# Products with V in two runs of three key tiles per unit, and the probabilities' copies split in halves

## The chip, the cores and the metric

One core of a Trainium2 chip. The metric is the time of one execution in device microseconds: the median of several runs. Beside the runs there is one execution with the hardware profiler on; its rows are what this document reads. PE is TensorE's matmul, PEld its weight load, DVE is VectorE, ACT is ScalarE, POOL is GpSimd, SP is SyncE. Lines (L406) are those of the kernel's file before the change.

## What is computed

A clustered attention and two feed-forward layers, one after the other. Only the first matters here:

```python
def _attn_ref(q, k, v, centroids):          # 2 batches, 8 heads, 768 positions, head width 64
    q_assign = np.argmax(np.einsum('bhsd,hcd->bhsc', q_n, c_n), axis=-1)
    k_assign = np.argmax(np.einsum('bhsd,hcd->bhsc', k_n, c_n), axis=-1)
    mask = q_assign[:, :, :, None] == k_assign[:, :, None, :]
    scores = scale * np.matmul(q, k.transpose(0, 1, 3, 2))
    scores = np.where(mask, scores, -1000000000.0)
    scores = scores - np.max(scores, axis=-1, keepdims=True)
    attn = np.exp(scores)
    attn = attn / (np.sum(attn, axis=-1, keepdims=True) + 1e-09)
    return np.matmul(attn, v)
```

Behind it, each token goes to one of eight experts (`moe`, 512 to 1024 to 512), and the result through a dense layer (`moe2`, 512 to 2048 to 512).

## The kernel before

The attention is cut into **units**: a unit is one pair of heads and one half (384) of the 768 query positions, so there are 2 x 4 x 2 = 16. A unit has six **steps**, one per head of the pair and per 128 queries (`part`, line 356). The loop at line 685 runs over all 96 steps and writes the order of the work out by hand; each engine takes its instructions in that order. For step `s` of the loop:

- `scores(s + 1)` (line 359): four matmuls on TensorE into `psS`, two for each stretch of keys (512 and 256 columns); lines 367 and 368 hold the product and the mask's part. `psS` has two buffers.
- `av(u - 1, [i])` (line 402): the products with V of the unit before, one **key tile** (128 of the 768 keys) per step, both heads, accumulated in `psO` over the six steps of a unit. In the trace these are four instructions of line 406 per key tile. After the sixth, `av_evac` (line 409) has ScalarE copy `psO` out (line 414).
- `rowmax(s + 1)` (line 372): VectorE's maximum over the 768 scores (line 374).
- `transp(s - 1)` (line 389): TensorE transposes the 128 x 768 probabilities in six 128 x 128 pieces into `psT` (line 396); then ScalarE copies the first four out (line 399), VectorE the last two (line 400). `psT` has one buffer.
- `softmax(s + 1)` (line 376): ScalarE's exponential with its row sum (line 384), which frees the buffer of `psS`.
- then whatever `todo` holds for that step: the preparation of the next pair of heads (`sim_pair` line 289, `simmax_pair` 301 with line 305 on TensorE and 307 on VectorE, `eqt_pair`, `first_pair`, `mask_pair`, VectorE's subtraction `qlo_pair` line 263, POOL's subtraction line 270), and, at steps 53 and 65 on, the routing of finished tokens (`Route`, line 419, with a product at line 456 and row transposes at line 536).

Unit 0 has no unit before it, so its steps have no products. Step 91 makes all six key tiles of unit 14 in one run (line 694). The last unit's products come in pieces of 128 queries near the end (lines 703, 733, 738).

All of PSUM is one tile `PS` of 4096 columns, eight stretches of 512:

```python
    PS = ps_a.tile([P, 4096], F32, name="PS")
    psS = [PS[:, 1024 * i:1024 * i + S] for i in range(2)]
    psT = PS[:, 2048:2048 + S]
    psO = PS[:, 3072:3072 + CH]
    psM = PS[:, 3584:4096]
```

So key tiles 0 to 3 of `psT` are columns 2048 to 2559, one stretch, and tiles 4 and 5 are in the next. `psM` is the scratch stretch of the preparation and the routing.

Of the kernel before, what the change touches and what calls it, by code (L numbers as in the profile page):

```python
# [14 lines left out]
AF = mybir.ActivationFunctionType  # L15
# [64 lines left out]
def tile_cluster_attention_moe(ctx: ExitStack, tc: tile.TileContext, qk, kk, v, cen, cenr, gate, mw, m2w,  # L80
                               alpha, consts, table, pos, zeros, out):
    nc = tc.nc
# [233 lines left out]
    def eqt_pair(p, hh=None):  # L316
        rs, _, ps = alone(p, hh)
        oh = pre["ohc"][1]
        pb = ps.bitcast(BF16)
        for t in range(3):  # L320
            nc.tensor.transpose(pb[rs, t * P:(t + 1) * P], oh[:, t * P + rs.start:t * P + rs.stop], idb)
        nc.scalar.activation(once("eT", p, [P, CH], BF16)[rs], pb[rs, :CH], AF.Copy)

    def first_pair(p, hh=None):
        rs, _, ps = alone(p, hh)
        eT = pre["eT"][1]
        if hh is not None:

            st, r0 = sets[p % 2], rs.start
            pk = (psT, psM)[hh]  # L330
            nc.tensor.matmul(pk[r0:r0 + 48, :CH], firstb[rs, r0 + NC:r0 + NC + 48], eT[rs], start=True, stop=True)
            nc.tensor.matmul(ps[rs, :CH], firstb[rs, rs], eT[rs], start=True, stop=True)
            for c in range(2):
                cs = slice(c * CH, (c + 1) * CH)
                r1 = r0 + 32 * c
                nc.scalar.activation(st["QB"][64:80, hh, cs], ps[r1:r1 + 16, :CH], AF.Relu)
                nc.vector.tensor_scalar(st["KB"][64:80, hh, cs], pk[r1:r1 + 16, :CH], 0.0, -NEG, ALU.is_le, ALU.mult)
            return
        nc.tensor.matmul(psM[:, :CH], firstb, eT, start=True, stop=True)
        pre["fr"] = ep.tile([P, CH], F32, name=f"fr_{p}", tag="fr")  # L340
        nc.scalar.activation(pre["fr"], psM[:, :CH], AF.Relu)
# [14 lines left out]
    def part(u, i):  # L356
        return (i % 3, i // 3) if u == 0 else divmod(i, 2)

    def scores(s):
        u, i = divmod(s, 6)  # L360
        qt, hh = part(u, i)
        p, c = divmod(u, 2)
        st = sets[p % 2]
        q0 = c * CH + qt * P
        ps = psS[s % 2]
        for ks in (slice(0, 512), slice(512, S)):
            nc.tensor.matmul(ps[:, ks], st["QA"][:, hh, q0:q0 + P], st["KA"][:, hh, ks], start=True, stop=False)  # L367
            nc.tensor.matmul(ps[:, ks], st["QB"][0:96, hh, q0:q0 + P], st["KB"][0:96, hh, ks], start=False, stop=True)  # L368
# [3 lines left out]
    def rowmax(s):  # L372
        smt[s] = sp.tile([P, 1], F32, name=f"sm_{s}", tag="sm")
        nc.vector.tensor_reduce(smt[s], psS[s % 2], AX.X, ALU.max, negate=True)  # L374

    def softmax(s):
        u, i = divmod(s, 6)
        qt, hh = part(u, i)
        p, c = divmod(u, 2)
        b, pr = divmod(p, NPAIR)  # L380
        tt = b * 6 + c * 3 + qt
        h = 2 * pr + hh
        Pt = pp.tile([P, S], F32, name=f"P_{s}", tag="P")
        nc.scalar.activation(Pt, psS[s % 2], AF.Exp, bias=smt.pop(s)[:, 0:1], accum_out=RS[:, tt, h:h + 1])  # L384
        Pts[s] = Pt

    PTs, OTt = {}, {}

    def transp(s):
        u, i = divmod(s, 6)  # L390
        qt, hh = part(u, i)
        Pt = Pts.pop(s)
        if i == 0:
            PTs[u] = ptp.tile([P, 2, KT, CH], F32, name=f"PT_{u}", tag="PT")
        for kt in range(KT):
            nc.tensor.transpose(psT[:, kt * P:(kt + 1) * P], Pt[:, kt * P:(kt + 1) * P], idf)  # L396
        v3 = psT.rearrange("p (k q) -> p k q", k=KT)
        qs = slice(qt * P, (qt + 1) * P)
        nc.scalar.activation(PTs[u][:, hh, 0:4, qs], v3[:, 0:4], AF.Copy)  # L399
        nc.vector.tensor_copy(PTs[u][:, hh, 4:6, qs], v3[:, 4:6])  # L400

    def av(u, kts, qs=slice(0, CH)):
        V = Vt[u // 2]
        for kt in kts:
            for hh in range(2):
                nc.tensor.matmul(psO[64 * hh:64 * hh + 64, qs], V[:, kt, 64 * hh:64 * hh + 64],  # L406
                                 PTs[u][:, hh, kt, qs], start=kt == 0, stop=kt == KT - 1)

    def av_evac(u, qs=slice(0, CH)):
        p, c = divmod(u, 2)  # L410
        b, pr = divmod(p, NPAIR)
        if (b, c) not in OTt:
            OTt[b, c] = otp.tile([P, NPAIR, CH], F32, name=f"OT_{b}_{c}", tag="OT")
        nc.scalar.activation(OTt[b, c][:, pr, qs], psO[:, qs], AF.Copy)
# [139 lines left out]
    def weave(*chains):  # L554

        def steps(parts):
            for f, *a in parts:
                g = f(*a)
                if hasattr(g, "__next__"):
                    yield from g  # L560
                yield
        left = [steps(c) for c in chains]
        while left:
            left = [g for g in left if next(g, left) is not left]
# [59 lines left out]
    U = NU - 1  # L624
# [60 lines left out]
    for s in range(NS):  # L685
        u, i = divmod(s - 1, 6)
        if s + 1 < NS:
            scores(s + 1)
        if 0 < u < U:
            av(u - 1, [i])  # L690
            if i == 5:
                av_evac(u - 1)
        elif u == U and i == 0:
            av(u - 1, range(KT))
            av_evac(u - 1)
        if s + 1 < NS:
            rowmax(s + 1)
        if s == 0:
            eqt_pair(0, 1)
            first_pair(0, 1)  # L700
        if s == NS - 3 or s == NS - 1:
            qs = slice((s - NS + 3) // 2 * P, (s - NS + 5) // 2 * P)
            av(U, range(KT), qs)
            av_evac(U, qs)
        if s > 0:
            transp(s - 1)
        if s + 1 < NS:
            softmax(s + 1)
        for f, a in todo.get(s, []):
            weave([(f, *a)])  # L710
        if s == NS - 5:
            ra = Route(1, 0, 0, 3, 2)
            weave([(ra.inv,), (ra.logits3,)])
        if s == NS - 4:
            weave([(ra.turn,), (ra.max,), (ra.exp,)])
        if s == NS - 3:
            weave([(ra.hot,)])
        if s == NS - 2:
            rb, rc = Route(1, 1, 0, 2, 3), Route(1, 1, 2, 3, 4, bank(1))
            ra.rankmm()  # L720
            ra.rowmm(0, bank(0))
            ra.rowmm(1, bank(1))
            weave([(ra.rankev,)], [(ra.gate,), (rb.inv,)])
            weave([(ra.rowev, 0, bank(0)), (ra.scatter, 0), (ra.rowev, 1, bank(1)), (ra.scatter, 1)])
    qs = slice(2 * P, CH)
    ra.rowmm(2, bank(2))
    rb.logits(ks=[0])
    rb.logits(ks=[1])
    weave([(rb.max,)])
    transp(NS - 1)  # L730
    rb.exp()
    rc.logits([0, 1, 2])
# [459 lines left out]
```

## Time and profile before

| | us |
|---|---|
| three runs: median (lowest to highest) | 749.64 (747.15 to 750.23) |
| the profiled execution: its time | 750.04 |
| its span, first to last instruction | 748.3 |
| what lies around the span | 1.74 |
| TensorE busy | 731.0 |
| VectorE busy | 408.3 |
| ScalarE busy | 291.0 |

The page gives busy times over the whole span. The attention loop ends at about 262 us; the expert and dense layers fill the rest. A row of a timeline gives the start in us, the duration of the (merged) instructions, engine, line, operation, output and inputs, shapes, how many, and in brackets the engine's idle time before it and what ended that. Ends of matmuls are modelled and neighbours overlap, so what a group of matmuls costs is read from start to start.

### The profile page before, as it was taken

The numbers are of one execution on the slowest core, as the hardware profiler recorded it, in microseconds if no ns is written. First come the engines' busy times: TensorE is split into PE (matmuls) and PEld (weight loads), VectorE is DVE, ScalarE is ACT, GpSimd is POOL, SyncE is SP. The second block draws the span as 40 slices with busy tenths as digits, with TensorE's granted clock in tenths as the row PEclk, the third lists the DMA queues.
The fourth block names the chain that finished last, engine by engine and source line by source line (L and its number), as shares of the span: only waits on it lengthen the run. The fifth ranks groups of instructions, "written<-read, shape, count | busy, mean of one in ns | idle before, by whom it ended". The sixth has DMA issues, their size and how long they took to land. (4 is left out here: it accounts for less than half of the span.)

```text
span 748.3 us, 10731 instructions
## 1 busy us (share of the span) xinstructions
PE 731.0 (98%) x4102; PEld 590.8 (79%) x4102; DVE 408.3 (55%) x774; ACT 291.0 (39%) x592; POOL 65.1 (9%) x69
## 2 busy tenths in 40 slices
PE   7999999999999999999999999799999999999996
PEld 2666666666666789999999999688888888888885
DVE  6866767677766540443423335499946343544332
ACT  3877777767666412222322223333312111211111
POOL 5120220222300120000000000000002000020002
PEclk8999999999999999999999999899999999999999
DMA  8265466343420037799786987233201000010001
GB/s 263 54 197 178 146 228 203 87 133 78 157 67 0 30 102 241 205 268 243 278 282 203 278 244 271 63 106 101 75 0 55 4 0 1 0 57 1 0 1 56
DMA packets 25284, 92.74 MB, mean 124 GB/s; under 512 B 7044, under 2 KB 8591, under 8 KB 20495
## 3 DMA queue, kind: packets, MB, share of 16 engines
q1 hardware_dynamic: 19815, 75.41, 32.9%
q0 software_dynamic: 3216, 12.60, 4.8%
q10 hardware_dynamic: 2200, 4.03, 2.0%
q8 instruction: 33, 0.54, 0.3%
q14 instruction: 20, 0.16, 0.1%
HBM read 78.04 MB, written 9.74 MB: 117 GB/s over the span
## 5 line engine op out<-in xcount | busy, mean ns | idle before, releaser
L848 PE MATMUL PS<-x,w 128*128 128x208 f32 (+1 forms) x576 | 108.9, 332 | 0.9 <-ACT h L850 0.9
L864 PE MATMUL PS<-h,w 128*128 128x208 f32 (+1 forms) x576 | 108.6, 332 | 0.0
L1079 ACT ACTIVATE gh<-gg 128x512 fp32r<-128x512 f32 x48 | 30.4, 632 | 193.3 <-DVE gg L1078 193.3
L374 DVE TENSOR_REDUCE sm<-PS 128x1 f32<-128x768 f32 x96 | 91.6, 954 | 23.7 <-PE PS L368 14.8
L396 PEld LDWEIGHTS PS<-cst,P 128*128 128x128 f32 x576 | 61.5, 140 | 51.8 <-ACT P L384 38.9
L848 PEld LDWEIGHTS PS<-x,w 128*128 128x128 f32 x576 | 98.3, 190 | 1.1 <-ACT h L850 1.1
L864 PEld LDWEIGHTS PS<-h,w 128*128 128x128 f32 x576 | 98.4, 190 | 0.0
L384 ACT ACTIVATE P<-PS,sm 128x768 f32<-128x768 f32 x96 | 86.0, 896 | 1.2 <-DVE sm L374 1.1
L396 PE MATMUL PS<-cst,P 128*128 128x128 f32 x576 | 83.6, 281 | 0.2 <-ACT PT L399 0.2
L406 PE MATMUL PS<-PT,V 128*64 128x384 f32 (+1 forms) x432 | 81.6, 471 | 0.0
L399 ACT ACTIVATE PT<-PS 128x512 f32<-128x512 f32 x96 | 57.4, 598 | 56.8 <-PE PS L396 55.4
L1067 PE MATMUL PS<-x2hi,w2h 128*128 128x512 f32 x192 | 75.9, 395 | 3.3 <-ACT x2hi L1055 3.3
L1077 DVE TENSOR_SCALAR gg<-PS,alph 128x512 f32<-128x512 f32 x48 | 36.0, 749 | 78.9 <-PE PS L1069 78.9
L1068 PE MATMUL PS<-x2lo,w2h 128*128 128x512 f32 x192 | 75.8, 395 | 0.0
L1069 PE MATMUL PS<-x2hi,w2l 128*128 128x512 f32 x192 | 75.6, 394 | 0.0
L1096 PE MATMUL PS<-w2h,gh 128*128 128x512 f32 x192 | 74.7, 389 | 0.0
L1097 PE MATMUL PS<-w2l,gh 128*128 128x512 f32 x192 | 74.7, 389 | 0.0
L1098 PE MATMUL PS<-w2h,gl 128*128 128x512 f32 x192 | 74.7, 389 | 0.0
L367 PE MATMUL PS<-KA,QA 128*128 128x512 f32 x192 | 74.0, 385 | 0.0
L850 ACT ACTIVATE h<-PS 128x208 f32<-128x208 f32 (+1 forms) x72 | 23.8, 334 | 121.8 <-PE PS L848 111.5
L400 DVE COPY PT<-PS 128x256 f32<-128x256 f32 x96 | 40.6, 423 | 46.9 <-PE PS L396 46.2
L368 PE MATMUL PS<-KB,QB 96*128 96x512 f32 x192 | 61.2, 340 | 0.0
(159 smaller groups left out, 865.3 us busy)
## 6 DMA issues: line engine op xcount, KB each, us to landing
w<-in_mw SPq DMA_DIRECT2D x36, 1024.0 KB
raw<-in_m2w SPq DMA_DIRECT2D x32, 512.0 KB
R<-in_qk SPq DMA_DIRECT2D x7, 768.0 KB
KA<-in_kk POOLq DMA_DIRECT2D x7, 768.0 KB
Xs<-in_zeros SPq DMA_DIRECT2D x8, 417.6 KB
xr<-Xs ACTq DMA_DIRECT2D x8, 417.6 KB
V<-in_v SPq DMA_DIRECT2D x8, 384.0 KB
QA<-QB SPq DMA_DIRECT2D x7, 384.0 KB
```

Source lines behind the costliest of these rows:

```text
L374: nc.vector.tensor_reduce(smt[s], psS[s % 2], AX.X, ALU.max, negate=True)
L384: nc.scalar.activation(Pt, psS[s % 2], AF.Exp, bias=smt.pop(s)[:, 0:1], accum_out=RS[:, tt, h:h + 1])
L396: nc.tensor.transpose(psT[:, kt * P:(kt + 1) * P], Pt[:, kt * P:(kt + 1) * P], idf)
L406: nc.tensor.matmul(psO[64 * hh:64 * hh + 64, qs], V[:, kt, 64 * hh:64 * hh + 64], PTs[u][:, hh, kt, qs], start=kt == 0, stop=kt == KT - 1)
L848: nc.tensor.matmul(ps, w[:, d, fs], x[:, d, :], start=d == 0, stop=d == 3)
L864: nc.tensor.matmul(yps[blk][o][:, 0:nb], w[:, f % 4, o * P:(o + 1) * P], h, start=f == 0, stop=f == 7)
L1067: nc.tensor.matmul(ps, whi[:, d, fs], xhi[:, d, :], start=d == 0, stop=False)
L1068: nc.tensor.matmul(ps, whi[:, d, fs], xlo[:, d, :], start=False, stop=False)
L1069: nc.tensor.matmul(ps, wlo[:, d, fs], xhi[:, d, :], start=False, stop=d == 3)
L1096: nc.tensor.matmul(y, gh[:, c], whi[:, f % 4, :], start=f == 0, stop=False)
L1097: nc.tensor.matmul(y, gh[:, c], wlo[:, f % 4, :], start=False, stop=False)
L1098: nc.tensor.matmul(y, gl[:, c], whi[:, f % 4, :], start=False, stop=f == 15)
```

## The change

Two edits. In `transp`, ScalarE copies three of the six transposed pieces and VectorE the other three. In the loop, a unit's products with V are issued at its third and its sixth step, three key tiles each time, instead of one at each step. Instructions and operands are otherwise the same.

```diff
@@ -396,8 +396,8 @@
             nc.tensor.transpose(psT[:, kt * P:(kt + 1) * P], Pt[:, kt * P:(kt + 1) * P], idf)
         v3 = psT.rearrange("p (k q) -> p k q", k=KT)
         qs = slice(qt * P, (qt + 1) * P)
-        nc.scalar.activation(PTs[u][:, hh, 0:4, qs], v3[:, 0:4], AF.Copy)
-        nc.vector.tensor_copy(PTs[u][:, hh, 4:6, qs], v3[:, 4:6])
+        nc.scalar.activation(PTs[u][:, hh, 0:3, qs], v3[:, 0:3], AF.Copy)
+        nc.vector.tensor_copy(PTs[u][:, hh, 3:6, qs], v3[:, 3:6])
 
     def av(u, kts, qs=slice(0, CH)):
         V = Vt[u // 2]
@@ -686,8 +686,9 @@
         u, i = divmod(s - 1, 6)
         if s + 1 < NS:
             scores(s + 1)
-        if 0 < u < U:
-            av(u - 1, [i])
+
+        if 0 < u < U and i % 3 == 2:
+            av(u - 1, range(i - 2, i + 1))
             if i == 5:
                 av_evac(u - 1)
         elif u == U and i == 0:
```

## Rows read from the trace of the kernel before

**Rows 1.** The page, part 1: busy us, share of the span, instructions.
```profile
PE 731.0 (98%) x4102; PEld 590.8 (79%) x4102; DVE 408.3 (55%) x774; ACT 291.0 (39%) x592; POOL 65.1 (9%) x69
```
**Rows 2.** Windows: length, busy PE, PEld, DVE, ACT, POOL, clock, DMA share, GB/s.
```profile
46.50:242.00 195.50, 195.50 (x1239) 125.27 (x1240) 136.76 (x247) 138.38 (x281) 32.65 (x30) 1.00 0.42 127
...
181.00:200.00 19.00, 19.00 (x131) 12.42 (x130) 14.85 (x38) 11.90 (x26) 3.95 (x6) 1.00 0.40 120
```
**Rows 3.** TensorE's timeline, a plain step: scores, products, transposes, next scores.
```profile
122.18 0.48 PE L367 MATMUL PS<-KA,QA 128*128 128x512 f32 x1
...
123.06 0.87 PE L406 MATMUL PS<-PT,V 128*64 128x384 f32 x4
123.86 0.87 PE L396 MATMUL PS<-cst,P 128*128 128x128 f32 x6
124.49 0.48 PE L367 MATMUL PS<-KA,QA 128*128 128x512 f32 x1
```
**Rows 4.** ScalarE's timeline, four stretches.
```profile
26.85 0.60 ACT L399 ACTIVATE PT<-PS 128x512 f32<-128x512 f32 x1
...
103.79 0.49 ACT L414 ACTIVATE OT<-PS 128x384 f32<-128x384 f32 x1 [0.26 <-PE PS L406]
...
111.43 0.90 ACT L384 ACTIVATE P<-PS,sm 128x768 f32<-128x768 f32 x1 [0.53 <-DVE sm L374]
...
124.55 0.60 ACT L399 ACTIVATE PT<-PS 128x512 f32<-128x512 f32 x1 [0.83 <-PE PS L396]
125.05 0.89 ACT L384 ACTIVATE P<-PS,sm 128x768 f32<-128x768 f32 x1
125.83 0.20 ACT L384 ACTIVATION_READ_ACCUMULATOR P<-PS,sm 128x1 f32 x1
```
**Rows 5.** VectorE's timeline, a step with preparation and the plain step.
```profile
108.28 0.56 DVE L307 TENSOR_REDUCE am<-PS 128x24 f32<-128x384 f32 x1
108.75 1.72 DVE L265 SCALAR_TENSOR_TENSOR QA<-R,QB 64x384 fp32r<-64x384 f32 x1
110.40 0.94 DVE L374 TENSOR_REDUCE sm<-PS 128x1 f32<-128x768 f32 x1
...
113.25 0.54 DVE L265 SCALAR_TENSOR_TENSOR QA<-R,QB 64x384 fp32r<-64x384 f32 x1
...
123.24 0.96 DVE L374 TENSOR_REDUCE sm<-PS 128x1 f32<-128x768 f32 x1 [0.36 <-PE PS L368]
124.77 0.42 DVE L400 COPY PT<-PS 128x256 f32<-128x256 f32 x1 [0.57 <-PE PS L396]
```
**Rows 6.** TensorE's timeline, the run of six key tiles and the step behind it.
```profile
242.73 4.09 PE L406 MATMUL PS<-PT,V 128*64 128x384 f32 x24
246.75 0.88 PE L396 MATMUL PS<-cst,P 128*128 128x128 f32 x6
247.56 0.85 PE L456 MATMUL PS<-OT,G 128*32 128x384 f32 x8
248.34 0.50 PE L367 MATMUL PS<-KA,QA 128*128 128x512 f32 x1
...
249.16 0.82 PE L396 MATMUL PS<-cst,P 128*128 128x128 f32 x6
249.81 0.49 PE L462 MATMUL PS<-cst,lt 128*128 128x128 f32 x3
```
**Rows 7.** Lines 307 and 400: ns min/median/max, first and last start; DVEq is the queue's sequencer.
```profile
L307 DVEq EVENT_SEMAPHORE  x9: 21/21/557, 10.3 to 202.4; - x9
L307 DVE TENSOR_REDUCE am<-PS x9: 340/558/559, 11.6 to 202.5; 128x24 f32<-128x384 f32 x7, 128x12 f32<-128x192 f32 x2
...
L400 DVE COPY PT<-PS x96: 403/424/427, 22.2 to 261.3; 128x256 f32<-128x256 f32 x96
```
**Rows 8.** TensorE's timeline in unit 0: the transposes of two steps without products.
```profile
25.41 0.88 PE L396 MATMUL PS<-cst,P 128*128 128x128 f32 x6
...
27.50 0.87 PE L396 MATMUL PS<-cst,P 128*128 128x128 f32 x6 [0.25 <-ACT PT L399]
```

## The prediction

> **What bounds the kernel now.** I read the page first: TensorE is busy for nearly all of the span [rows 1]. [...] The timeline then has to show that TensorE really issues one thing after the other. In a plain step the scores start at 122.18, the products with V at 123.06, the transposes at 123.86, the next scores at 124.49 [rows 3]: 0.88 + 0.80 + 0.63 = 2.31 us, and the next transposes never wait for the copies out of `psT`. ScalarE starts its copy 0.69 us after the first transpose and VectorE 0.91 us after it [rows 4, 5]; the two run at once, on different 512-column stretches of PS, and end 1.29 and 1.33 us after the first transpose. The next transposes come 2.31 us after. So about 1 us of slack hides the copies, and TensorE's own order sets the pace.
>
> **Products in runs of three.** The stretch at 242.73 is what the change makes more of: the six key tiles of unit 14 in one run take 246.75 - 242.73 = 4.02 us [rows 6], against 0.80 for one tile alone [rows 3]. Each further tile of a run costs (4.02 - 0.80)/5 = 0.64 us. A step without products shows behind it: scores at 248.34, transposes at 249.16, what follows them at 249.81 [rows 6]: 1.47 us, so one tile costs 2.31 - 1.47 = 0.84 in a step of its own, 0.20 of it for going over to the products and back. A step with three tiles takes 2.31 + 2 x 0.64 = 3.60. Three steps cost 3 x 2.31 = 6.93 now, and 3.60 + 2 x 1.47 = 6.54 if nothing waits: 0.39 less. Units 1 to 14 hold 28 such threes: **-10.9 us**, on TensorE, which is the path.
>
> **The copies in halves.** This gives 128 of the columns from ScalarE to VectorE. ScalarE's copy of 384 columns takes 0.49 instead of 0.60 (the row of line 414 has that form) [rows 4]. VectorE's, 0.42 for 256 columns, has no row of 384: below is 0.42, above half as much again, 0.64; I take 0.56, which line 307's reduction over 384 columns of PSUM took [rows 5].
>
> The larger matter is a wait that the trace of before has no instance of. Key tiles 0 to 3 lie in one 512-column stretch of PS, tiles 4 and 5 in the next. Now each copy has a stretch to itself. After the change VectorE reads tile 3 in the stretch from which ScalarE reads tiles 0 to 2. Do they still run at once? Unordered, the copies cost nothing (VectorE's ends 0.91 + 0.56 = 1.47 after the first transpose, and only tiles 3 to 5 wait for it). Ordered, VectorE starts when ScalarE has ended, and the next first transpose waits for both. I take ordered, by a weak sign: line 307, VectorE's first read of `psM`, into a tile that VectorE alone uses, has an extra semaphore wait on its queue nine times in nine, and ScalarE is who read `psM` before it; line 400, alone on its stretch, has none in 96 [rows 7].
> [...]
>
> Priced from rows, from one first transpose to the next: 0.69 to ScalarE's start, 0.49 copy, 0.05 handover, 0.56 copy, 0.05 handover = 1.84 us. The handover is that from ScalarE's copy (26.85 + 0.60 = 27.45) to the transposes waiting for it (27.50) [rows 4, 8]. A step without products needs 1.47, so TensorE stands 0.37 in each of 56 such steps: **+20.7**. Bounds: 0.30 with VectorE's copy at 0.49 like ScalarE's, 0.45 at 0.64, so +16.8 to +25.2. In the step with three tiles (3.60) the copies stay hidden.
>
> **What covers part of it.** TensorE's other work between transposes fills the wait. Of each of the six pairs prepared in units 1 to 12, one step without products has three transposes more (estimate 0.32, half of the six's 0.63 [rows 3]) and another one small product (estimate 0.15). Each of the two routing groups has a product of 0.78 (247.56 to 248.34 [rows 6]), two steps with four row transposes (0.42 each) and one with a few rank matmuls (0.15). Capped at 0.37 a step: 6 x 0.47 + 2 x 1.26 = 5.3: **-5.3**, an estimate, with -3 if those of VectorE's making come too late to fill the wait, and -6.5 if the last bits in the other steps count too.
>
> **What VectorE adds.** A step without products gives VectorE a row maximum of 0.96 and the copy of 0.56 in 1.84. Where line 307's reduction and line 265's subtraction (0.56 and 0.54) join, it needs 2.62 and is 0.78 late [rows 5]. Queued behind it are the next row maximum, for which the exponential waits, and the next copy. From nothing to 6 x 0.78 = 4.7. I take **+1.8**, nearer nothing, since a subtraction of 1.72 us at 108.75 [rows 5] left TensorE's steps at their length in the trace of before. Unit 0 has no products at all: transposes start at 25.41 and 27.50 [rows 8], the second already after a wait for ScalarE's copy; VectorE's copy behind it costs 0.1 to 1.3, I take **+0.9**. In the last four steps one pair of transposes has nothing between: **+0.4** (0 to 0.8).
>
> Not moved: the output copy of line 414 stays after tile 5, V's loads keep their step and their two buffers, no DMA is issued elsewhere; SP's and POOL's queues keep their order. Line 265 shares the time with POOL's subtraction of line 270; where they meet may shift, within the +1.8.
>
> **Sum**: -10.9 + 20.7 - 5.3 + 1.8 + 0.9 + 0.4 = +7.6 us on the profiled execution's 750.04, which stands 0.40 above the median of the runs, 749.64: 757.2 against that median. What follows the loop starts later by as much and is no shorter. A measurement here can tell about 0.5% from no change: 745.9 to 753.4 is the same.
>
> **Rivals.** A, *copies unordered* (0.16): faster. The 0.37 falls away, but another limit appears: two score buffers. From scores to row maximum 1.06 us, then 0.96, handover 0.09 (111.34 to 111.43), exponential with its read-out 0.78 + 0.20, handover 0.05 [rows 3, 4, 5]: 3.14 until that buffer takes scores again, against 2 x 1.47 = 2.94 for two steps without products. 0.20 x 28 = 5.6 is given back: -10.9 + 5.6 + 1.0 for VectorE and unit 0 = -4.3, 745.7. It decides if VectorE's copy starts before ScalarE's ends. For it: the two overlap now [rows 4, 5]. Against: they don't touch one stretch now.
>
> B, *ordered, but only tile 3 waits for VectorE* (0.08): no change. Tile 3 is written some 0.33 after tile 0, so a first transpose needs 1.84 - 0.33 = 1.51, 0.04 over: -10.9 + 2.2 + 5.6 + 1.8 + 0.9 + 0.4 = 0.0, 750.0. Against it: waits would have to be kept tile by tile within a stretch.
>
> C, *VectorE becomes the bound* (0.05): slower still, with its terms at their upper ends: 20.7 - 10.9 - 5.3 + 4.7 + 1.3 + 0.8 = +11.3, 761.3. For it: in routing steps VectorE is busy 14.85 of 19 us [rows 2]; against: the step with three tiles gives 1.8 us of rest each time.
>
> **The numbers.** The forecast has 0.71, and its own range is 753 to 762: of it 0.65 is slower by over 0.5%, 0.06 within, where the wait is cheaper or better covered. A ends near the edge: 0.11 faster, 0.05 the same. B: 0.07 the same, 0.01 slower. C: slower. Together 0.11, 0.18, 0.71. The range is 745.3 to 762.0: it takes in A, the cases between and most of C.
>
> **What would show it.** In the profile after: line 400 at 128x384, some 0.56 us, started by ScalarE's line 399 and no longer by TensorE's line 396; TensorE's weight loads of line 396 idle for some 15 to 20 us with line 400 as releaser; starts of the transposes 1.84, 1.84 and 3.60 apart in a unit without preparation; runs of 12 line-406 matmuls in about 2.1 us. Line 400 starting before line 399 ends would be A. Starts 1.5 apart with ordered copies would be B. Runs of well over 2.1 us would break the first term.

## Result and the profile after

The changed kernel takes 754.87 us (median of 6 runs) beside 748.67 us for the kernel before in the same series: a ratio of 1.0082 [1.0058, 1.0106]. That is slower by 0.8%, beyond the 0.5% that a measurement here can tell. The forecast was 757.2, slower, with a range of 745.3 to 762.0. One of the six runs, at 828.52 us and a granted clock of 0.844 (0.990 to 0.992 in the other five), is left out of the ratio (the median of the other five is 754.56).

The profiled execution took 753.58 us (span 751.8). The page's part 1 of the changed kernel, which answers to [rows 1]: busy us, share of the span, instructions.

```profile
PE 724.1 (96%) x4102; PEld 594.7 (79%) x4102; DVE 413.0 (55%) x774; ACT 282.8 (38%) x592; POOL 64.6 (9%) x69
```

TensorE has less work (724.1 instead of 731.0 us: the runs of three), and yet the span is longer. The windows view over the stretch of [rows 2] says where; its columns are those of [rows 2].

```profile
46.50:242.00 195.50, 185.90 (x1218) 126.99 (x1210) 139.01 (x246) 129.06 (x275) 32.51 (x30) 1.00 0.43 128
```

TensorE, busy in every microsecond of this stretch before, now stands for 195.50 - 185.90 = 9.6 us of it, at the same granted clock of 1.00. What ended these gaps stands in the page's part 5 of the changed kernel (line, engine, operation, out<-in, count | busy us, mean ns | idle us before, and the releaser of most of it):

```profile
L396 PE MATMUL PS<-cst,P 128*128 128x128 f32 x576 | 83.4, 281 | 11.2 <-DVE PT L400 10.6
L396 PEld LDWEIGHTS PS<-cst,P 128*128 128x128 f32 x576 | 61.7, 141 | 39.6 <-DVE PT L400 22.1
...
L400 DVE COPY PT<-PS 128x384 f32<-128x384 f32 x96 | 53.3, 555 | 64.7 <-ACT PT L399 59.3
```

Two releasers are new. The transposes (line 396) wait for VectorE's copy (line 400), 10.6 us on TensorE itself, and VectorE's copy waits for ScalarE's (line 399) instead of for the transposes. One plain unit shows both. TensorE's timeline of the changed kernel, to be read beside [rows 3]:

```profile
120.08 0.87 PE L396 MATMUL PS<-cst,P 128*128 128x128 f32 x6
...
121.91 0.88 PE L396 MATMUL PS<-cst,P 128*128 128x128 f32 x6 [0.24 <-DVE PT L400]
...
123.74 0.88 PE L396 MATMUL PS<-cst,P 128*128 128x128 f32 x6 [0.24 <-DVE PT L400]
...
125.25 2.16 PE L406 MATMUL PS<-PT,V 128*64 128x384 f32 x12
127.34 0.88 PE L396 MATMUL PS<-cst,P 128*128 128x128 f32 x6
```

ScalarE's timeline there, beside [rows 4], and VectorE's, beside [rows 5]:

```profile
124.43 0.49 ACT L399 ACTIVATE PT<-PS 128x384 f32<-128x384 f32 x1 [0.17 <-PE PS L396]
```

```profile
123.12 0.56 DVE L400 COPY PT<-PS 128x384 f32<-128x384 f32 x1
...
124.96 0.56 DVE L400 COPY PT<-PS 128x384 f32<-128x384 f32 x1 [0.41 <-ACT PT L399]
```

Follow one round. Transposes start at 123.74; ScalarE copies from 124.43, 0.69 later, to 124.92; VectorE starts at 124.96, 0.04 after that end, though the transposes end at 123.74 + 0.88 = 124.62. The copy of the round before ended at 123.12 + 0.56 = 123.68, and the transposes started 0.06 later. The period is 1.83 us where no products stand between, twice per three steps; the third takes 127.34 - 123.74 = 3.60, with a run of three tiles in 2.09. So the two copies out of one stretch stand in order here, 0.04 us apart; what an unordered pair would do, no run here shows.

For the rest I count from the start of one step's scores to that of another (the first line-367 product of a step in TensorE's timeline, steps counted from 0), in us:

| kernel | whole loop, 0 to 92 | unit 0, 0 to 8 | plain unit, 83 to 89 | one pair's preparation, 11 to 23 | the same, 32 to 44 | routing, 53 to 62 | tail, 92 to the last transposes |
|---|---|---|---|---|---|---|---|
| before | 225.80 | 15.51 | 13.88 | 29.44 | 29.44 | 24.88 | 18.24 |
| changed | 231.74 | 16.32 | 14.53 | 29.67 | 29.67 | 26.53 | 18.68 |
| runs alone | 220.97 | 15.59 | 13.56 | 28.40 | 28.31 | 24.79 | 18.24 |
| halves alone | 228.09 | 16.70 | 13.88 | 29.63 | 30.10 | 24.88 | 18.68 |
| two stretches | 222.38 | 15.96 | 13.52 | 28.55 | 28.48 | 25.31 | 18.37 |
| runs of two, two stretches | 215.66 | 15.68 | 13.13 | 27.99 | 27.75 | 24.38 | 18.38 |

Loop and tail are 5.94 + 0.44 = 6.4 us longer, and the medians differ by 754.87 - 748.67 = 6.2. The two profiled executions differ by only 753.58 - 750.04 = 3.5, because the changed one came to its first scores 1.05 us sooner (14.99 instead of 16.04) and needed 1.8 us less behind the loop, where the change touches nothing.

### The profile page after: what moved, and what is told of

It is laid out like the page before. It is cut to its first block, busy times and chain, and to the rows that moved or that the text cites. A ratio compares the mean times of both kernels' runs of the same rounds, so it can differ in the third digit from the quotient of the medians.

```text
span 751.8 us, 10931 instructions
## 1 busy us (share of the span) xinstructions
PE 724.1 (96%) x4102; PEld 594.7 (79%) x4102; DVE 413.0 (55%) x774; ACT 282.8 (38%) x592; POOL 64.6 (9%) x69
## 5 line engine op out<-in xcount | busy, mean ns | idle before, releaser
L396 PE MATMUL PS<-cst,P 128*128 128x128 f32 x576 | 83.4, 281 | 11.2 <-DVE PT L400 10.6
L396 PEld LDWEIGHTS PS<-cst,P 128*128 128x128 f32 x576 | 61.7, 141 | 39.6 <-DVE PT L400 22.1
L400 DVE COPY PT<-PS 128x384 f32<-128x384 f32 x96 | 53.3, 555 | 64.7 <-ACT PT L399 59.3
L406 PE MATMUL PS<-PT,V 128*64 128x384 f32 (+1 forms) x432 | 69.3, 458 | 0.0
L399 ACT ACTIVATE PT<-PS 128x384 f32<-128x384 f32 x96 | 46.8, 488 | 40.8 <-PE PS L396 38.4
```

## The experiments

My theory: the runs of three save TensorE's time, and the copies in halves cost more than that, because both read one 512-column stretch of PS and so run one after the other. The rivals: the runs themselves cost (a third limit behind them), or VectorE has too much to do.

**One part alone.** The changed kernel with the old copies:

```diff
-        nc.scalar.activation(PTs[u][:, hh, 0:3, qs], v3[:, 0:3], AF.Copy)
-        nc.vector.tensor_copy(PTs[u][:, hh, 3:6, qs], v3[:, 3:6])
+        nc.scalar.activation(PTs[u][:, hh, 0:4, qs], v3[:, 0:4], AF.Copy)
+        nc.vector.tensor_copy(PTs[u][:, hh, 4:6, qs], v3[:, 4:6])
```

> Products in runs of three as in the change, copies as before (ScalarE four tiles, VectorE two, each alone on its stretch of PS). Theory (the loss comes from VectorE's copy being ordered behind ScalarE's): faster than before by about 5 us, ratio 0.993; the ideal 10.9 us is not reached, because scores, row maximum and exponential take 3.14 us until a score buffer is free and two steps without products offer 2.94. VectorE's line 400 is released by line 396 and the transposes' weight loads never by line 400. Rival 1 (runs of three themselves cost: the two steps without products are too short for VectorE and ScalarE, whatever the copies): no gain or slower, ratio 1.000 to 1.008.

Measured: 742.77 us, 0.9920 [0.9901, 0.9939] of before; the loop is 4.83 us shorter. Its groups of lines in the stretch 46.5 to 242 (columns as in part 5):

```profile
L396 PEld LDWEIGHTS PS<-cst,P 128*128 128x128 f32 x468 | 51.8, 141 | 17.9 <-issue 15.5 <-ACT PT L399 1.5 <-ACT P L384 0.6
...
L400 DVE COPY PT<-PS 128x256 f32<-128x256 f32 x79 | 32.9, 416 | 43.7 <-PE PS L396 43.7
```

The transposes wait for line 400 no more, and line 400 is released by the transposes again. The runs of three by themselves are a gain of 0.8%.

The other part alone, in the kernel before:

```diff
-        nc.scalar.activation(PTs[u][:, hh, 0:4, qs], v3[:, 0:4], AF.Copy)
-        nc.vector.tensor_copy(PTs[u][:, hh, 4:6, qs], v3[:, 4:6])
+        nc.scalar.activation(PTs[u][:, hh, 0:3, qs], v3[:, 0:3], AF.Copy)
+        nc.vector.tensor_copy(PTs[u][:, hh, 3:6, qs], v3[:, 3:6])
```

> Copies in halves as in the change, one key tile of products per step as before. Theory: the two copies are ordered, 1.83 us from a first transpose to the next, but a step with one key tile has 2.31 us, so TensorE waits in unit 0 and in the last steps alone (some 1.3 us) and a little where VectorE is crowded (0 to 2): +1 to +3.5 us, ratio 1.002 to 1.005. Rival 2 (the halves cost VectorE time that matters in every step, 96 x 0.13 us): +12 us, ratio 1.016.

Measured: 752.12 us, 1.0036 [1.0022, 1.0050]; the loop is 2.29 us longer. The waits of this kernel from 32 to 250 us (us in total, times, longest):

```profile
DVE PT L400 <- ACT PT L399: 44.0, 64, 0.9
```

The order is there with one product per step too, but a plain unit takes 13.88 as before: a step of 2.31 us has room for a round of 1.84. The loss lies in unit 0 (16.70 instead of 15.51) and in steps where VectorE has other work: at 114.21 the transposes wait 0.60 us for line 400, which stands behind a subtraction (line 265) of 2.09 us. The parts don't add: -4.83 + 2.29 = -2.5 for the loop, and together they make +5.94. The runs take away the cover under which the ordered copies cost little.

**The order undone.** The same halves, but the transposed tiles of the two engines lie in different 512-column stretches, so that neither engine's work changes:

```diff
+    psT2 = PS[:, 2048:3072]
...
-            nc.tensor.transpose(psT[:, kt * P:(kt + 1) * P], Pt[:, kt * P:(kt + 1) * P], idf)
-        v3 = psT.rearrange("p (k q) -> p k q", k=KT)
+            c0 = 512 * (kt // 3) + P * (kt % 3)
+            nc.tensor.transpose(psT2[:, c0:c0 + P], Pt[:, kt * P:(kt + 1) * P], idf)
+        va = psT2[:, 0:CH].rearrange("p (k q) -> p k q", k=3)
+        vb = psT2[:, 512:512 + CH].rearrange("p (k q) -> p k q", k=3)
...
-        nc.scalar.activation(PTs[u][:, hh, 0:3, qs], v3[:, 0:3], AF.Copy)
-        nc.vector.tensor_copy(PTs[u][:, hh, 3:6, qs], v3[:, 3:6])
+        nc.scalar.activation(PTs[u][:, hh, 0:3, qs], va, AF.Copy)
+        nc.vector.tensor_copy(PTs[u][:, hh, 3:6, qs], vb)
```

> The change with one thing undone: transposed tiles 0 to 2 lie in one 512-column stretch of PS and tiles 3 to 5 in the next, so each half copy has its own stretch; sizes of the copies and runs of three stay. Theory: the wait of line 400 for line 399 is gone, ratio to before 0.993 to 0.995 (-4 to -5 us), some 10 us below the change. Rival 3 (VectorE's longer copy makes the loss, not the order): stays at 1.006 to 1.010.

Measured: 745.79 us, 0.9957 [0.9941, 0.9973], a little less gain than expected. ScalarE's and VectorE's timelines of this kernel (transposes are line 398 here, the copies 402 and 403):

```profile
123.84 0.49 ACT L402 ACTIVATE PT<-PS 128x384 f32<-128x384 f32 x1 [2.31 <-PE PS L398]
```

```profile
124.17 0.56 DVE L403 COPY PT<-PS 128x384 f32<-128x384 f32 x1 [1.86 <-PE PS L398]
```

VectorE starts at 124.17, before ScalarE ends at 124.33, and is released by the transposes. VectorE has the same copies to make as in the changed kernel, and the plain unit falls from 14.53 to 13.52. So it is mainly the shared stretch that costs. Of the 0.0162 between runs alone (0.9920) and the change (1.0082) it makes 0.0125, some 9.4 us. The other 0.0037, some 2.8 us, the halves cost without it: 745.79 against 742.77 in one series, by the table most of it in unit 0 and at routing.

**Only tile 3 behind ScalarE.** VectorE's three tiles in the changed kernel, in two copies, the free stretch first:

```diff
-        nc.vector.tensor_copy(PTs[u][:, hh, 3:6, qs], v3[:, 3:6])
+        nc.vector.tensor_copy(PTs[u][:, hh, 4:6, qs], v3[:, 4:6])
+        nc.vector.tensor_copy(PTs[u][:, hh, 3:4, qs], v3[:, 3:4])
```

> The change, with VectorE's copy in two instructions: first tiles 4 and 5, alone on their stretch, then tile 3, which shares ScalarE's. Theory: only the piece for tile 3 (some 0.29 us) is ordered behind ScalarE's copy, so a first transpose can follow 0.69 + 0.49 + 0.03 + 0.29 + 0.05 = 1.55 us after the last, 0.08 over a step without products instead of 0.37: about 56 x 0.28 = 16 us less wait, of which the score buffers give back 5 and VectorE's extra instruction (0.2 us in each of 96 steps) some 2 to 4: 744 to 749 us, ratio 0.994 to 1.001. Rival (the longer VectorE time per step makes the loss): slower than the change, above 1.009.

Measured: 749.39 us, 1.0012 [0.9994, 1.0030], just above what was expected. TensorE's and VectorE's timelines of this kernel:

```profile
123.86 0.88 PE L396 MATMUL PS<-cst,P 128*128 128x128 f32 x6
...
125.45 0.88 PE L396 MATMUL PS<-cst,P 128*128 128x128 f32 x6
```

```profile
124.77 0.42 DVE L400 COPY PT<-PS 128x256 f32<-128x256 f32 x1 [1.93 <-PE PS L396]
125.11 0.28 DVE L401 COPY PT<-PS 128x128 f32<-128x128 f32 x1
```

The copy of tiles 4 and 5 is released by the transposes; it starts at 124.77, 0.91 us after the first transpose, and the period falls from 1.83 to 1.59 us: what lies outside the shared stretch did not wait for ScalarE. A third way to the same finding, and no gain over the kernel before.

**Where the cover lies.** The table holds a misfit. A stretch of 12 steps with one pair's preparation has four threes; at the plain unit's (14.53 - 13.88)/2 = 0.325 each it should have grown by 1.30, and it grew by 0.23. I had counted a piece of preparation in the step that issues it. TensorE's timeline of the changed kernel there:

```profile
104.95 0.87 PE L396 MATMUL PS<-cst,P 128*128 128x128 f32 x6
105.75 0.85 PE L296 MATMUL PS<-R,CB 128*32 128x384 f32 x8
106.53 0.50 PE L367 MATMUL PS<-KA,QA 128*128 128x512 f32 x1
...
107.36 0.82 PE L396 MATMUL PS<-cst,P 128*128 128x128 f32 x6
108.01 0.49 PE L305 MATMUL PS<-cst,sT 128*128 128x128 f32 x3
...
109.22 0.87 PE L396 MATMUL PS<-cst,P 128*128 128x128 f32 x6
```

The product of line 296 (106.53 - 105.75 = 0.78 us) is issued at the end of a step with products, but it stands in front of the next scores, so it fills the next wait: the transposes are 2.41 and then 1.86 apart, both without a wait. The mended theory says that preparation covers by its place among the steps, modulo three. So I moved it (one line, with another number each time):

```diff
-        s0 = max(12 * (p - 1), 1)
+        s0 = 12 * (p - 1) + 2 if p > 1 else 1
```

> The change, with the preparation of pairs 2 to 7 two steps later, so that its first piece of TensorE work falls on the second step without products instead of the step with three tiles. Theory, mended (work added at the end of a step lies in front of the next scores, so it covers the wait of the next step's transposes; it counts if the next step has no products): now 0.37 + 0.25 + 0.17 + 0.1 = 0.9 us of wait is covered per pair, later 0.25 + 0.1: +3.2 us over the change for six pairs, and up to 4 more where VectorE's work of the preparation meets two tight steps: 758 to 762 us, ratio 1.012 to 1.017. Rival (as the prediction counted it: work covers the wait of the step in which it is issued): 0.5 us per pair covered either way, no difference from the change within 1 us.

> The change, with the preparation of pairs 2 to 7 three steps later: the same place against the runs of products as in the change, but another half of the unit. Both theories: within 2 us of the change, ratio 1.006 to 1.011. If it is as slow as the kernel with two steps, lateness of the preparation and not its place against the runs makes the difference.

Measured, two steps later: 775.32 us, 1.0352 [1.0310, 1.0393]; three later: 781.07, 1.0438 [1.0411, 1.0465]. Both totals are far above what either theory gave, so as totals they are misses. The waits of the first over its whole loop name one cause that has nothing to do with the copies:

```profile
PE PS L368 <- DMA KB<-E: 4.3, 2, 2.2
```

The mask rows of KB, prepared later, arrive after the scores that need them. That is 4.3 us of the 256.49 - 231.74 = 24.8 by which its loop is longer than the changed kernel's. Routing's products (lines 456 and 462) wait another 6.4 us for ScalarE's work of the preparation, and line 396 waits 14.7 us for line 400 instead of 10.6. Then there is the clock. TensorE's timeline behind the first wait for KB, and a row of the windows view (columns of [rows 2]):

```profile
76.49 0.47 PE L368 MATMUL PS<-KB,QB 96*128 96x512 f32 x1 [2.13 <-DMA KB<-E]
...
77.13 3.60 PE L406 MATMUL PS<-PT,V 128*64 128x384 f32 x12
80.66 1.07 PE L396 MATMUL PS<-cst,P 128*128 128x128 f32 x6
```

```profile
78.00:80.00 2.00, 2.00 (x10) 0.68 (x6) 0.20 (x1) 0.00 (x0) 0.00 (x0) 0.50 1.03 415
```

The run of three tiles takes 80.66 - 77.13 = 3.53 us instead of 2.09, at a granted clock of 0.50. Over loop and tail TensorE is busy for 247.1 us with the 1593 instructions that took 237.6 in the changed kernel. What can be read is the stretch from step 11 to 23, which has no such wait and a clock of 1.00 in all three: 30.70 us with preparation two steps later, 29.66 with three, 29.67 in the changed kernel. A shift by three, which keeps the place, costs nothing there, and a shift by two costs 1.03. From 32 to 44 the shift by two costs 1.74, of it 0.66 a wait for a transfer.

The other direction keeps the transfers early; one step earlier is the same place, modulo three, as two steps later. Once with the ordered copies and once with the old ones, the second as the control:

```diff
-        s0 = max(12 * (p - 1), 1)
+        s0 = 12 * (p - 1) - 1 if p > 1 else 1
```

> The change, with the preparation of pairs 2 to 7 one step earlier, so that nothing of it comes late: its large product is then issued in the second step without products, in front of the step with three tiles. Mended theory (TensorE work at the end of a step covers the wait of the next step's transposes, if that step has no products): of 0.9 us covered per pair about 0.35 is left, and VectorE's reduction and subtraction, which now meet the step with three tiles, cost nothing more or up to 0.5 per pair: +3 to +6 us over the change, 758 to 761 us, ratio 1.012 to 1.017. Rival (work covers the wait of the step in which it is issued): 0.5 us per pair either way, 1.007 to 1.010 like the change.

> The same earlier preparation with the copies of before (four tiles and two, each alone on its stretch) and runs of three: there is no wait for VectorE's copy that other work could cover. Mended theory: within 2 us of the run with runs of three alone, ratio 0.991 to 0.995. If the earlier preparation is slow by itself (a late transfer, a buffer still in use), it is slow here too: above 0.998.

Measured: 768.42 us, 1.0258 [1.0238, 1.0277] with halves, and 754.02, 1.0065 [1.0050, 1.0080] with the old copies. Again both totals miss: earlier preparation is slow by itself, as the control shows (754.02 against 742.77 for the same copies with preparation in its place). In the control TensorE waits 2.18 us for a transfer (R, line 296, until 44.61), and the granted clock is 0.50 behind it. The difference between the two is the test, in a stretch with a clock of 1.00. From step 32 to 44 the halves lose 30.92 - 29.67 = 1.25 us by the shift, the old copies 29.02 - 28.31 = 0.71. That leaves 0.54 for this one pair, where the mended theory gave 0.55 and its rival none. The hit is in part luck. VectorE's and TensorE's timelines of the kernel with halves there:

```profile
118.66 0.55 DVE L307 TENSOR_REDUCE am<-PS 128x24 f32<-128x384 f32 x1
...
119.85 0.94 DVE L374 TENSOR_REDUCE sm<-PS 128x1 f32<-128x768 f32 x1
120.72 0.54 DVE L400 COPY PT<-PS 128x384 f32<-128x384 f32 x1
```

```profile
118.80 0.88 PE L396 MATMUL PS<-cst,P 128*128 128x128 f32 x6
...
121.31 0.87 PE L396 MATMUL PS<-cst,P 128*128 128x128 f32 x6 [0.93 <-DVE PT L400]
```

These transposes are 2.51 us apart, 0.65 more than the 1.86 of the changed kernel, because line 400 stands on VectorE's queue behind the reduction, a subtraction and the row maximum. I had expected this work to meet the step with three tiles; it met a step without products. With the old copies the shift leaves this step at its length (1.69 against 1.70). The run of three and the step behind it, which the product of line 296 covers or not, lose 0.38 by the shift with the halves and 0.13 with the old copies. So 0.25 of the 0.54 is cover lost, 0.66 is VectorE's queue, and in the other steps the old copies lose 0.37 more than the halves. That the place of the preparation matters is shown; that all of the 0.54 is lost cover is not.

**Shorter runs.** If a round of copies is hidden whenever products stand in the step, runs of two tiles alternate a covered step with an uncovered one. Once with the old copies and once with the halves on two stretches (as above); in both:

```diff
-        if 0 < u < U and i % 3 == 2:
-            av(u - 1, range(i - 2, i + 1))
+        if 0 < u < U and i % 2 == 1:
+            av(u - 1, range(i - 1, i + 1))
```

> Copies as before (four tiles by ScalarE, two by VectorE, each alone on its stretch), products in three runs of two key tiles per unit. Theory (going over to the products and back is what a run saves, 0.20 us each time, and score buffers cost only where two steps without products follow each other): 42 x 0.20 = -8.4 us, with unit 0 untouched: ratio 0.986 to 0.990, better than runs of three with the same copies (0.992). Rival (VectorE and ScalarE are too slow for any step without products): no better than 0.992.

Measured: 743.09 us, 0.9920 [0.9900, 0.9941], a miss: no better than runs of three with these copies. TensorE's and ScalarE's timelines of this kernel:

```profile
127.56 0.88 PE L396 MATMUL PS<-cst,P 128*128 128x128 f32 x6
...
128.98 0.82 PE L396 MATMUL PS<-cst,P 128*128 128x128 f32 x6
...
129.88 0.47 PE L367 MATMUL PS<-KA,QA 128*128 128x512 f32 x1
```

```profile
128.25 0.60 ACT L399 ACTIVATE PT<-PS 128x512 f32<-128x512 f32 x1 [1.59 <-PE PS L396]
128.75 0.90 ACT L384 ACTIVATE P<-PS,sm 128x768 f32<-128x768 f32 x1
129.53 0.20 ACT L384 ACTIVATION_READ_ACCUMULATOR P<-PS,sm 128x1 f32 x1
```

The scores that could follow the transposes of 128.98 by 0.63, as in [rows 3], follow by 0.90. They need the score buffer that the exponential reads, and the exponential stands on ScalarE's queue behind the copy of four tiles: it starts at 128.75, ends its read-out at 129.73, and the scores start at 129.88. This is the limit of two score buffers that rival A priced, now made later by the copy.

> As the run with two stretches, with products in three runs of two key tiles per unit, in every second step. Theory: per two steps 2.31 + 0.64 + 1.47 = 4.42 instead of 4.62, 42 times: -8.4 us, and no two steps without products follow each other, so the score buffers (3.14) never wait: ratio 0.986 to 0.990. Rival 1 (steps without products are too short for VectorE and ScalarE): little better than runs of three, ratio 0.993 to 1.000.

Measured: 739.05 us, 0.9866 [0.9849, 0.9883], the fastest kernel of the study and 1.3% below the kernel before. TensorE's timeline (products are line 409 here):

```profile
121.37 0.88 PE L398 MATMUL PS<-cst,P 128*128 128x128 f32 x6
...
122.79 0.82 PE L398 MATMUL PS<-cst,P 128*128 128x128 f32 x6
...
124.34 1.51 PE L409 MATMUL PS<-PT,V 128*64 128x384 f32 x8
125.78 0.87 PE L398 MATMUL PS<-cst,P 128*128 128x128 f32 x6
```

Two steps take 1.42 + 2.99 = 4.41 us instead of 2 x 2.31 = 4.62. A copy of three tiles (0.49) lets ScalarE come to the exponential sooner than one of four (0.60): its read-out ends at 123.32 and the scores start at 123.47, 0.68 after the transposes and, as with four tiles, 0.15 after the read-out. So with runs of two the halves are worth having, once each engine reads a stretch of its own (0.9866 against 0.9920); with runs of three they are not (0.9957 against 0.9920).

## Why the prediction was right

**Runs of three** (-10.9). Right: 12 line-406 matmuls take 2.09 us, the step 3.60, both as worked out. What they give when nothing is ordered is less than 10.9, by the two score buffers: a three costs 13.52/2 = 6.76 with two stretches and 13.56/2 = 6.78 with the old copies, where rival A had 6.54 + 0.20 = 6.74. A's whole price, -4.3, was for what the kernel with two stretches does, which took 745.79 beside 749.14 in its series, -3.35. TensorE's timeline and its weight loads in that kernel:

```profile
119.24 1.01 PE L398 MATMUL PS<-cst,P 128*128 128x128 f32 x6
```

```profile
120.26 0.19 PEld L368 LDWEIGHTS PS<-KA,QA 128*128 128x128 f32 x1 [0.25 <-ACT P L385]
```

The scores follow the transposes by 1.02 us instead of 0.63, and the exponential (line 385 here) releases them.

**Copies ordered** (+20.7). Right in kind and size. Line 400 took 0.555 us (taken: 0.56, from line 307's row); the period is 1.83 (worked out: 1.84); the releasers are those named, and the weight loads of line 396 idle 22.1 us for line 400 (forecast: 15 to 20). The weak sign of [rows 7] pointed the right way: in the changed kernel line 400 has the extra semaphore wait on its queue 96 times in 96, and in the kernel with two stretches its copy has none.

```profile
L400 DVEq EVENT_SEMAPHORE  x96: 21/21/21, 20.8 to 266.6; - x96
```

Both terms together: a plain three grew by 0.325, times 28 is +9.1, against -10.9 + 20.7 = +9.8.

**Unit 0** (+0.9) **and tail** (+0.4). Measured +0.81 and +0.44 in the table.

**Cover and crowding** (-5.3 and +1.8) came out near in sum by luck, and wrong in their parts; this is the step that failed. Measured, their sum is 6.38 - 9.1 - 0.81 - 0.44 = -4.0, against -3.5. But preparation covers 1.30 - 0.23 = 1.07 per pair (measured for the two pairs of the table; -6.4 if all six do), where I had counted 0.47: "one step without products has three transposes more". I had left out the product of line 296, as issued in a step with products, though it stands ahead of the next scores. That its place matters is shown by the shifts. Routing I had at -1.26 per group. It costs instead: steps 47 to 83, which hold three pairs and both groups, grew by 2.75, where three pairs make 0.69, so +2.06. VectorE's timeline of the changed kernel in such a step, and TensorE's:

```profile
152.85 0.54 DVE L265 SCALAR_TENSOR_TENSOR QA<-R,QB 64x384 fp32r<-64x384 f32 x1
153.31 0.34 DVE L469 TENSOR_TENSOR lh<-PS,RI 128x192 f32<-128x192 f32 x1
153.69 0.54 DVE L476 TENSOR_REDUCE lg<-lh 128x24 f32<-128x192 f32 x1
...
154.58 0.95 DVE L374 TENSOR_REDUCE sm<-PS 128x1 f32<-128x768 f32 x1
155.45 0.55 DVE L400 COPY PT<-PS 128x384 f32<-128x384 f32 x1
```

```profile
152.99 0.88 PE L396 MATMUL PS<-cst,P 128*128 128x128 f32 x6
...
156.05 0.87 PE L396 MATMUL PS<-cst,P 128*128 128x128 f32 x6 [1.47 <-DVE PT L400]
```

Routing's reductions and the row maximum stand in front of line 400, which starts at 155.45, and the transposes are 3.06 apart instead of 1.83. With runs alone steps 53 to 62 don't grow (24.79 against 24.88), though the three from 56 to 59 does, by 0.63 there and by 1.24 in the changed kernel: about half of this crowding comes with the runs, whatever the copies. So the crowding that I put at line 307 sits mostly at routing. A rest sits in steps 23 to 35, which grew by 0.61 instead of 0.23: line 265's subtraction took 2.19 us there (at 79.47; 0.80 at 109.55, in steps 32 to 44), and line 400 came late behind it. Together -6.4 + 2.06 + 0.38 = -4.0.

**The rivals.** A fell with line 400's releaser, B with the 1.83 between transposes: the wait was for the whole of VectorE's copy, and only a copy cut in two brought it near B. C fell too: VectorE is busy for 139.01 of 195.50 us, hardly more than before, and with the same copies on two stretches the kernel is faster than before.

**Not tried:** the exponential ahead of the copy on ScalarE's queue, and routing moved away from the steps without products.

## What to carry to other kernels

When work in PSUM is split between two reading engines, try the split at the 512-column stretch (move the tiles if need be): here the two reads of one stretch came one after the other, 0.04 us apart, and the same halves on two stretches took 745.79 us instead of 754.87. Before products are gathered into runs, look at what they hid: the steps left without products have to hold the whole round of copies by themselves (here 1.83 us, in steps that need 1.47 without a wait [rows 6]). Count covering work where it stands in TensorE's queue, which is in front of the next step's scores, and not in the step that issues it; and count what stands in front of the copy on the copying engine's queue.

## What was not expected of the hardware

- The gaps of the changed kernel cost no clock: with 9.6 us of TensorE's idle time spread over 195.5 us, the granted clock stayed at 1.00. Behind the waits of 2.13 and 2.18 us in the kernels with shifted preparation it was 0.50; what sets it, no run here shows.
- Going over to the products and back had a fixed price here. Runs of one, two and three tiles took 0.80 [rows 3], 125.78 - 124.34 = 1.44 and 2.09 us, some 0.64 for each further tile, so the first carries 0.16 more. What makes up the 0.16, no run here tells.
- A step without products took 1.42 us where nothing waited (runs of two on two stretches) (122.79 - 121.37), a little less than the 1.47 of [rows 6].
